# Shared key and value buffers in a sliding-window attention kernel, and output weights split by adding transfers

## The chip, the core and the metric

The kernel runs on one NeuronCore of a Trainium2 chip. The core has a matrix engine (TensorE, PE in the profile, with PEld for its weight loads), a vector engine (VectorE, DVE), a scalar engine (ScalarE, ACT), a general engine (GpSimd, POOL) and a sequencer for transfers (SyncE, SP). Transfers are issued in order from the queues of SP, ACT and POOL and are carried out by 16 DMA engines. The metric is the time of one execution on the device in microseconds (us); lower is better.

## What is computed

The input `x` has 2048 tokens of 512 channels. Two branches are computed from it and mixed by a gate for each token.

```python
q, k, v = split(x @ wqkv)                 # 32 heads of 16 channels
idx = pos[:, None] - off[None, :]         # 8 keys per token, 2 apart, back in time
logits = einsum("bhsd,bhswd->bhsw", q, k[idx]) * scale   # masked where idx < 0
a = einsum("bhsw,bhswd->bhsd", softmax(logits), v[idx]) @ wo
b = (gelu(x @ w_gate) * (x @ w_up)) @ w_down             # hidden width 1792
g = sigmoid((x * gate_w).sum(-1))
out = g * a + (1 - g) * b
```

All numbers are 32 bit floats.

## The kernel before

**Precision.** TensorE multiplies a rounded format, `float32r`. Each operand is split into a high part (the rounded number, a copy on ACT) and a low part (number minus high part), and each product is made of three matmuls: high by high, low by high, high by low. The low part is made in one of two ways. `split` (L83) and `lo` (L787) subtract on DVE. `operands` (L376) and `down_w` (L415) do it with a transfer: ACT writes the negated, rounded number into the place of the low part, and a transfer from POOL's queue adds the full number to it (`accum_op=add`); what is left is the low part.

**Parities.** Since the keys of a token are 2, 4, ... 14 tokens back, even and odd tokens never meet in the attention. The kernel treats them as two parities, 0 and 1, of 1024 tokens each, one behind the other: `start` makes the keys and queries of parity 0, `ffn(0)` runs the hidden layer of parity 0, `kq_second` makes keys and queries of parity 1, and `ffn(1)` runs the hidden layer of parity 1, `out_first` the output product of parity 0, and `finish` that of parity 1. The matmuls of keys and queries and of the hidden layer are arranged as 2 by 2 blocks with seven products in place of eight (names `t1` to `t4`, `s1` to `s4`).

**The hidden layer.** `ffn(par)` goes over 14 blocks `f` of weights. For each, the weights are fetched by SP (`fetch`, L356; in parity 1 the sums made before come back by `fetch_sums`, L409), combined on DVE (`combine`, L367), and split (`operands`). `gate_up` (L494) makes the products of the block; `copy`, `add` and `hidden` (L435 to L450) take them from the PSUM banks. `down` (L464) multiplies pairs of finished blocks by the down weights. In the first two blocks of each parity the values of the attention are made as well (`values`, L174, stored by `take`, L158, through staging tiles `hh`, `hl` and `c`).

**The attention.** It runs on DVE, with its exponential on ACT, beside the matmuls. Each parity has four units `u` of 8 heads (128 channels). A partition holds 8 tokens of a parity in a row and the 7 before them, so keys and values of a unit have 15 slots of 128 channels and queries have 8. For each unit:

- `load_kq` (L185) loads keys (two transfers, `load_slots`, L195) and queries (one) from DRAM into a tile `kq` of 23 slots. For unit 0 they are there already: `take_first` (L137) copies them from PSUM straight into the tile, and `shift` (L148) fetches the 7 earlier slots from the neighbouring partition, after a memset of the first partition's on POOL.
- `scores` (L207) makes four products of 2048 columns (L212) and sums (L215) into `lg`, of which there are two buffers.
- `softmax` (L223), `gated` (L239), and `mix` (L249), which loads the values into a tile `v` of 15 slots, makes four products (L260) with their sums (L264 to L268) into `o`, transposes on DVE into `tb` (L273) and stores to DRAM (L275).

Tiles come from a pool. `kq`, `v`, `tb` and `prod` have one buffer each, so each new tile of such a name waits until all readers of the last one are done. In `start` the buffers of `v`, `tb` and `prod` hold raw weights.

**What sets the order.** `attention` (L296) is a generator that lists the units' steps, each with a price in us; `pull` (L338) is called between the matmuls and takes as many steps as its budget pays for. The steps get a lower priority than the matmuls' own work (`BEHIND`, 150 places), and the products L212 and L260 are tied to the matmul last issued (`paced`). From priorities, dependencies and a simulated timeline a scheduler then sets the order on each engine and each queue; there is no order written out by hand for the attention.

The attention's list begins with `load_kq(0, 0)`, `scores(0, 0)`, `load_kq(0, 1)`, `scores(0, 1)`. After that the next unit's loads come ahead of a unit's `mix` and its scores behind it. At the parity's border the list is: `load_kq(1, 0)`, `scores(1, 0)`, `load_kq(1, 1)`, `softmax(1, 0)`, `scores(1, 1)`.

**The output weights.** `fetch_o` (L649) loads `wo` from POOL's queue during the last block but one of parity 1. `load_o` (L655) splits its four chunks (`WO[u]`) in the last block, with `split` on DVE, into a buffer `g1` (chunks 0 and 1) and two pairs of `S`. `channels_of` and `channels` (L666, L680) then load and split the attention's result, also with `split`; `by_unit` (L689) makes the output's matmuls at L693.

Of the kernel before, what the change touches and what calls it, by code (L numbers as in the profile page):

```python
# [10 lines left out]
F32 = mybir.dt.float32  # L11
F32R = mybir.dt.float32r
AF = mybir.ActivationFunctionType
OP = mybir.AluOpType
AX = mybir.AxisListType

P = 128
# [31 lines left out]
def tile_gated_mix(ctx: ExitStack, tc: tile.TileContext, xt, wqkv, wff, wo, out):  # L49
# [33 lines left out]
    def split(eng, hi, lo, raw, copy=None):  # L83
        if copy:
            copy(hi, raw)
        else:
            nc.scalar.activation(hi, raw, AF.Copy)
        eng.tensor_tensor(lo, raw, hi.bitcast(F32), op=OP.subtract)
# [47 lines left out]

    def take_first(par, ps, jj, copy):  # L137

        if par not in KQ:
            KQ[par] = pool.tile([P, 3 * NP - 1, UC], F32, name="kq")  # L140
        st = tl(next(stages))[:, :CU].rearrange("p (a d) -> p a d", a=2)
        two = ps.rearrange("p (a c d) -> p c a d", a=2, c=2)
        copy(KQ[par][:, NP - 1 + jj::NP], two[:, 0])
        copy(st, two[:, 1])
        for a, t in enumerate((KS[par, 0][1, W:], QS[par, 0][1])):
            nc.sync.dma_start(t.rearrange("(p j) d -> j p d", j=NP)[jj], st[:, a])

    def shift(par, queue, i, j):  # L148
        k = KQ[par][:, :2 * NP - 1]
        if not i:  # L150
            nc.gpsimd.memset(k[:1, :NP - 1], 0.0)
        for a, b in (1, P - 15), (P - 15, P):
            queue.dma_start(k[a:b, i:j], k[a - 1:b - 1, NP + i:NP + j])
# [28 lines left out]

    LG = {}

    def load_kq(par, u):  # L185
        hh, c = divmod(u, 2)
        kq = KQ[par] if not u else pool.tile([P, 3 * NP - 1, UC], F32, name="kq")
        k, q = kq[:, :2 * NP - 1], kq[:, 2 * NP - 1:]
        LG[par, u] = k, q
        if not u:  # L190
            return
        load_slots(k, KS[par, hh][c])
        nc.sync.dma_start(q, QS[par, hh][c].rearrange("(p j) d -> p j d", j=NP))
# [13 lines left out]
    def scores(par, u):  # L207
        k, q = LG[par, u]
        lg = pool.tile([P, UH, NP, W], F32, name="lg", bufs=2)
        for jj in range(0, NP, 2):  # L210
            prod = pool.tile([P, 2, W, UC], F32, name="prod")
            paced(nc.vector.tensor_tensor(prod, spans(k, jj), q[:, jj:jj + 2, None, :].to_broadcast([P, 2, W, UC]),  # L212
                                          op=OP.mult))
            yield 2.3
            nc.vector.tensor_reduce(two_of(lg, jj), prod.rearrange("p j w (h d) -> p (j w) h d", d=DH), axis=AX.X,  # L215
                                    op=OP.add)
            yield 2.3
        first = lg[:1, :, :NP - 1, :W - 1]
        nc.vector.tensor_tensor(first, first, mask[:1, None, :NP - 1, :W - 1].to_broadcast([1, UH, NP - 1, W - 1]),
                                op=OP.min)  # L220
        LG[par, u] = lg
# [27 lines left out]
    def mix(par, u, pause):  # L249
        lg = LG.pop((par, u))  # L250
        hh, c = divmod(u, 2)
        v = pool.tile([P, 2 * NP - 1, UC], F32, name="v")
        load_slots(v, VS[par, hh][c])
        yield pause
        tb = pool.tile([P, 2, BT * UC], F32, name="tb")
        for jj in range(0, NP, 2):
            if jj % BT == 0:
                o = pool.tile([P, 4, BT, 32], F32, name="o")
            prod = pool.tile([P, 2, W, UC], F32, name="prod")
            paced(nc.vector.tensor_tensor(prod.rearrange("p j w (h d) -> p (j w) h d", d=DH),  # L260
                                          spans(v, jj).rearrange("p j w (h d) -> p j w h d", d=DH),
                                          two_of(lg, jj)[:, :, :, None].to_broadcast([P, 2 * W, UH, DH]), op=OP.mult))
            yield 2.3
            nc.vector.tensor_tensor(prod[:, :, :4], prod[:, :, :4], prod[:, :, 4:], op=OP.add)  # L264
            yield 1.2
            nc.vector.tensor_tensor(prod[:, :, :2], prod[:, :, :2], prod[:, :, 2:4], op=OP.add)
            two = [prod[:, :, i].rearrange("p j (b c) -> p b j c", b=4) for i in range(2)]
            nc.vector.tensor_tensor(o[:, :, jj % BT:jj % BT + 2], *two, op=OP.add)  # L268
            yield 1.1

            if jj % BT == BT - 2:
                t = tb[:, jj // BT]
                nc.vector.transpose(t, o.rearrange("p b t c -> p (b t c)"))  # L273
                for a in range(4):
                    nc.sync.dma_start(OS[par, u, jj // BT][:, :, a].rearrange("b i c -> i b c"),  # L275
                                      t[32 * a:32 * a + 32].rearrange("p (b c) -> p b c", b=4))
                yield 0.7
# [18 lines left out]
    def attention():  # L296
        units = [(0, u) for u in range(NU)] + [(1, u) for u in range(NU)]
        yield from need(0, 0)
        load_kq(0, 0)
        yield from scores(0, 0)  # L300
        load_kq(0, 1)
        yield from scores(0, 1)
        yield from need(0, 1)
        scored, mixed = 2, False
        for i, un in enumerate(units):
            if scored == i:
                yield from need(un[0], un[1] // 2 * 2)
                load_kq(*un)
                if un[1]:
                    yield LOAD  # L310
                yield from scores(*un)
                scored += 1
                mixed = False
            if un == (1, 0):
                load_kq(*units[scored])
            yield from softmax(*un)
            if un == (1, 0):
                yield from scores(*units[scored])
                scored += 1
                yield from need(un[0], 1)  # L320
            yield from gated(*un)


            to = units[scored] if scored < len(units) else None
            ahead = to and (to[0], to[1] // 2 * 2) in done
            if ahead:
                load_kq(*to)
            yield from mix(*un, LOAD if mixed else 0.0)
            done.add((*un, "o"))
            mixed = not ahead  # L330
            if ahead:
                yield from scores(*to)
                scored += 1
# [101 lines left out]
    def copy(ps):  # L435
        s = tl("s")
        COPIED[:] = [nc.scalar.activation(s, ps, AF.Copy)]  # L437
        return s
# [216 lines left out]
    def load_o():  # L655
        t = tl("g1", F32R)
        cols = [t[:, i * 512:(i + 1) * 512] for i in range(4)]
        for u in range(NU):
            raw = WO[u]
            WO[u] = hi, lo = pair("S") if u > 1 else cols[2 * u:2 * u + 2]  # L660
            split(nc.vector, hi, lo, raw)
            yield

    OR = []
# [580 lines left out]
```

## Time and profile before

| | |
|---|---|
| median of 3 runs | 600.98 us (600.16 to 601.4) |
| the profiled execution, its own time | 602.86 us |
| its span, first to last instruction | 601.0 us |
| granted TensorE clock | 1.00 |
| TensorE matmul, weight load | 591.8 us (98%), 493.1 us (82%) |
| VectorE | 531.1 us (88%) |
| ScalarE | 391.9 us (65%) |
| GpSimd | 89.3 us (15%) |
| DMA | 134.18 MB, mean 223 GB/s |

How to read it: busy times are of one profiled execution. The span is shorter than the execution's own time by what lies before the first and behind the last instruction. Most waits of an engine other than TensorE cost nothing as long as TensorE is busy meanwhile. Names on the left of an arrow are the tile written, names on its right the tile read; `kq<-ks` is a key load, `kq<-qs` a query load, `v<-vs` a value load, `os<-tb` a store of the attention's result, `raw<-wff` a fetch of hidden weights, `g<-raw` and `d<-r` the making of their parts. L760 is the line of a helper through which many operations of `start` and `kq_second` go.

### The profile page before, as it was taken

How to read it: one execution, taken by the hardware profiler on the slowest of the kernel's cores; microseconds unless marked ns; L12 is line 12 of the kernel's file. 1: busy time of each engine (PE TensorE's matmuls, PEld its weight loads, DVE VectorE, ACT ScalarE, POOL GpSimd, SP SyncE). 2: the span in 40 equal slices, each digit the busy share in tenths (PEclk: the TensorE clock that was granted, in tenths of full speed). 3: DMA queues.
4: the chain of work that ended last, by engine and by line, in shares of the span. 5: the costliest groups of instructions: out<-in, count | busy, mean ns of one | idle time of the engine just before them, and what ended most of it. 6: DMA issues, size and time to landing. Idle time of an engine off the chain costs nothing.

```text
span 601.0 us, 8207 instructions
## 1 busy us (share of the span) xinstructions
PE 591.8 (98%) x2778; PEld 493.1 (82%) x2778; DVE 531.1 (88%) x618; ACT 391.9 (65%) x670; POOL 89.3 (15%) x121
## 2 busy tenths in 40 slices
PE   8999999999999999999999999999999999999997
PEld 6889987788888787888889988788888888888886
DVE  5997969999898897899989887999999988799862
ACT  6845657787678766787772375667667656885532
POOL 0501001111111111202026001111111111101300
PEclk9999999999999999999999999999999999999999
DMA  8789896999889989887879858597867877648924
GB/s 318 259 250 248 242 266 187 265 256 249 241 241 258 232 236 253 223 262 279 282 221 302 219 155 282 144 245 195 238 172 216 214 226 171 168 106 227 159 68 155
DMA packets 80449, 134.18 MB, mean 223 GB/s; under 512 B 8092, under 2 KB 46362, under 8 KB 80152
## 3 DMA queue, kind: packets, MB, share of 16 engines
q1 hardware_dynamic: 62890, 97.67, 50.3%
q0 software_dynamic: 12576, 32.97, 27.5%
q10 hardware_dynamic: 4942, 3.01, 1.6%
q8 instruction: 22, 0.36, 0.3%
q14 instruction: 19, 0.16, 0.1%
HBM read 68.30 MB, written 38.86 MB: 178 GB/s over the span
## 4 chain that ended last, share of the span: by engine, by line
PE 65%; DMA 12%; issue 11%; DVE 7%; ACT 2%; SPq 1%; POOL 1%; ACTq 0%; POOLq 0%; DVEq 0%
PE p L432 26%; PE p L475 9%; PE acc L475 8%; PE acc L760 6%; PE p L693 5%; PE p L760 5%; PE acc L130 4%; DMA d<-r 3%; DMA kq<-qs 3%; DMA ws<-g 3%; DVE prod L212 3%; PE acc L693 2%; DVE lg L215 1%; DMA g<-raw 1%; DMA vs<-hl 1%
## 5 line engine op out<-in xcount | busy, mean ns | idle before, releaser
L432 PE MATMUL p<-S,g 128*128 128x512 f32 x672 | 166.8, 390 | 0.5 <-ACT s L437 0.4
L432 PEld LDWEIGHTS p<-S,g 128*128 128x128 f32 x672 | 125.4, 188 | 27.2 <-ACT s L437 0.8
L432 PE MATMUL p<-A,g 128*128 128x512 f32 x504 | 127.2, 390 | 0.1
L432 PEld LDWEIGHTS p<-A,g 128*128 128x128 f32 x504 | 94.1, 188 | 20.6 <-DVE c L442 1.1
L212 DVE TENSOR_TENSOR prod<-kq 128x2048 f32<-128x2048 f32 x32 | 73.1, 2284 | 16.6 <-DMA kq<-qs 7.7
L390 POOL DMA_DIRECT2D g<-raw x40 | 34.6, 865 | 300.5 <-ACT g L389 230.1
L260 DVE TENSOR_TENSOR prod<-v,lg 128x2048 f32<-128x2048 f32 x32 | 72.9, 2277 | 2.3 <-DMA v<-vs 1.4
L215 DVE TENSOR_REDUCE lg<-prod 128x128 f32<-128x2048 f32 x32 | 73.0, 2281 | 0.2
L475 PE MATMUL p<-d,hh 128*128 128x512 f32 x224 | 68.1, 390 | 0.3 <-ACT hh L448 0.3
L475 PE MATMUL acc<-d,hh 128*128 128x512 f32 x224 | 60.7, 391 | 1.8 <-DMA d<-r 1.8
L475 PEld LDWEIGHTS acc<-d,hh 128*128 128x128 f32 x224 | 41.8, 188 | 11.6 <-DMA d<-r 2.6
L475 PEld LDWEIGHTS p<-d,hh 128*128 128x128 f32 x224 | 42.0, 188 | 9.5 <-ACT hh L448 0.8
L394 ACT ACTIVATE g<-raw 128x1024 fp32r<-128x1024 f32 (+1 forms) x40 | 39.5, 989 | 13.4 <-PE p L432 13.4
L389 ACT ACTIVATE g<-raw 128x1024 fp32r<-128x1024 f32 (+1 forms) x40 | 39.4, 985 | 10.9 <-PE p L760 4.6
L442 DVE TENSOR_TENSOR c<-p,s 128x512 f32<-128x512 f32 x56 | 38.0, 681 | 9.2 <-PE p L432 8.4
L448 ACT ACTIVATE hh<-c 128x512 fp32r<-128x512 f32 x56 | 35.0, 625 | 15.5 <-DVE c L446 15.0
L437 ACT ACTIVATE s<-p 128x512 f32<-128x512 f32 x56 | 33.1, 593 | 18.0 <-PE p L432 16.5
L475 PE MATMUL p<-d,hl 128*128 128x512 f32 x112 | 42.7, 390 | 1.0 <-DVE hl L449 1.0
L449 DVE TENSOR_TENSOR hl<-c,hh 128x512 fp32r<-128x512 f32 x56 | 38.3, 683 | 3.1 <-ACT hh L448 3.0
L446 DVE TENSOR_TENSOR c<-c 128x512 f32<-128x512 f32 x56 | 38.2, 682 | 2.1 <-ACT c L543 1.8
L264 DVE TENSOR_TENSOR prod<-prod 128x1024 f32<-128x1024 f32 x32 | 39.0, 1218 | 0.3
L491 ACT ACTIVATE rt<-p 128x512 f32<-128x512 f32 x48 | 28.2, 593 | 15.3 <-PE p L475 15.2
(180 smaller groups left out, 929.5 us busy)
## 6 DMA issues: line engine op xcount, KB each, us to landing
g<-raw POOLq DMA_DIRECT2D x27, 512.0 KB, 6.8
raw<-wff SPq DMA_DIRECT2D x42, 256.0 KB, 3.4
ws<-g SPq DMA_DIRECT2D x14, 768.0 KB, 6.1
g<-ws SPq DMA_DIRECT2D x14, 768.0 KB, 5.5
r<-wff SPq DMA_DIRECT2D x28, 256.0 KB, 4.3
d<-r POOLq DMA_DIRECT2D x24, 256.0 KB, 6.9
g<-raw POOLq DMA_DIRECT2D x13, 384.0 KB, 6.0
v<-vs SPq DMA_DIRECT2D x8, 512.0 KB, 5.7
```

The source lines that it names most:

```text
L212: paced(nc.vector.tensor_tensor(prod, spans(k, jj), q[:, jj:jj + 2, None, :].to_broadcast([P, 2, W, UC]), op=OP.mult))
L215: nc.vector.tensor_reduce(two_of(lg, jj), prod.rearrange("p j w (h d) -> p (j w) h d", d=DH), axis=AX.X, op=OP.add)
L260: paced(nc.vector.tensor_tensor(prod.rearrange("p j w (h d) -> p (j w) h d", d=DH), spans(v, jj).rearrange("p j w (h d) -> p j w h d", d=D ...
L264: nc.vector.tensor_tensor(prod[:, :, :4], prod[:, :, :4], prod[:, :, 4:], op=OP.add)
L389: nc.scalar.activation(lo, raw, AF.Copy, scale=-1.0)
L394: ins = nc.scalar.activation(hi, raw, AF.Copy)
L432: LAST[:] = [nc.tensor.matmul(ps, w_, a_, start=(start and kc == 0 and n == 0), stop=(kc == 1 and n == 2), skip_group_check=True)]
L446: nc.vector.tensor_tensor(ge, ge, up, op=OP.mult)
L449: nc.vector.tensor_tensor(hl_, ge, hh_.bitcast(F32), op=OP.subtract)
L475: ins = nc.tensor.matmul(pp, a[:, ts], w, start=(i == 0 and n == 0 and gr == 0), stop=(i == 1 and n == 2), skip_group_check=True)
L693: ins = nc.tensor.matmul(pa, a, b, start=(first and n == 0), stop=(last and n == 2), skip_group_check=True)
L760: return lambda *args, **kw: self.add(getattr(self.eng, name)(*args, **kw))
```

## The change

It has two parts.

**Shared buffers.** There are two lasting tiles in place of one per load: `KQ["a"]` of 23 slots (named `kq`) and `KQ["b"]` of 15 slots (named `v`). Keys of unit 0 are in `a` and those of units 1 to 3 in `b`. Queries are in `a`'s last 8 slots, but those of unit 1 go into a `tb` tile. Values of units 0 to 2 are loaded into `a`'s first 15 slots and those of unit 3 into `b`. With this `load_kq(par, 1)` stands ahead of `scores(par, 0)` in the list, in both parities. Parity 1's first keys and queries are copied into the same tile `a` as parity 0's.

**Output weights.** `load_o` makes the low part of each chunk as `operands` does: a negating copy on ACT, an adding transfer from POOL, then the high copy on ACT; the subtraction on DVE goes.

```diff
     def take_first(par, ps, jj, copy):
 
-        if par not in KQ:
-            KQ[par] = pool.tile([P, 3 * NP - 1, UC], F32, name="kq")
+        if "a" not in KQ:
+            KQ["a"] = pool.tile([P, 3 * NP - 1, UC], F32, name="kq")
...
-        copy(KQ[par][:, NP - 1 + jj::NP], two[:, 0])
+        copy(KQ["a"][:, NP - 1 + jj::NP], two[:, 0])
...
     def shift(par, queue, i, j):
-        k = KQ[par][:, :2 * NP - 1]
+        k = KQ["a"][:, :2 * NP - 1]
...
+    def slots_of(other):
+        if not other:
+            return KQ["a"][:, :2 * NP - 1]
+        if "b" not in KQ:
+            KQ["b"] = pool.tile([P, 2 * NP - 1, UC], F32, name="v")
+        return KQ["b"]
+
     def load_kq(par, u):
         hh, c = divmod(u, 2)
-        kq = KQ[par] if not u else pool.tile([P, 3 * NP - 1, UC], F32, name="kq")
-        k, q = kq[:, :2 * NP - 1], kq[:, 2 * NP - 1:]
+        k, q = slots_of(u > 0), KQ["a"][:, 2 * NP - 1:]
+        if u == 1:
+            q = pool.tile([P, 2, BT * UC], F32, name="tb").rearrange("p a (b c) -> p (a b) c", c=UC)
...
     def mix(par, u, pause):
         lg = LG.pop((par, u))
         hh, c = divmod(u, 2)
-        v = pool.tile([P, 2 * NP - 1, UC], F32, name="v")
+        v = slots_of(u == NU - 1)
         load_slots(v, VS[par, hh][c])
...
         yield from need(0, 0)
         load_kq(0, 0)
+        load_kq(0, 1)
         yield from scores(0, 0)
-        load_kq(0, 1)
         yield from scores(0, 1)
...
                 if un[1]:
                     yield LOAD
+                else:
+                    load_kq(un[0], 1)
                 yield from scores(*un)
...
-            if un == (1, 0):
-                load_kq(*units[scored])
             yield from softmax(*un)
...
             WO[u] = hi, lo = pair("S") if u > 1 else cols[2 * u:2 * u + 2]
-            split(nc.vector, hi, lo, raw)
+            nc.scalar.activation(lo, raw, AF.Copy, scale=-1.0)
+            nc.gpsimd.dma_start(lo.bitcast(F32), raw, accum_op=OP.add)
+            nc.scalar.activation(hi, raw, AF.Copy)
             yield
```

## The prediction

> **What bounds the kernel now.** I read the page's totals first, then the 15 us windows, the waits of TensorE, and the timelines of DVE, ACT, POOL and SP around the places that the change touches.
>
> ```profile
> span 601.0 us, 8207 instructions
> PE 591.8 (98%) x2778; PEld 493.1 (82%) x2778; DVE 531.1 (88%) x618; ACT 391.9 (65%) x670; POOL 89.3 (15%) x121
> ...
> 75.00:90.00 15.00, 14.58 (x72) 12.06 (x72) 10.23 (x12) 7.66 (x14) 0.85 (x1) 1.00 0.92 262
> 90.00:105.00 15.00, 14.66 (x65) 11.59 (x64) 14.98 (x20) 10.91 (x16) 2.54 (x3) 1.00 0.67 194
> 195.00:210.00 15.00, 14.38 (x64) 11.59 (x63) 13.23 (x18) 10.73 (x17) 2.57 (x3) 1.00 0.92 234
> 225.00:240.00 15.00, 13.85 (x61) 11.18 (x60) 11.82 (x11) 10.27 (x16) 2.57 (x3) 1.00 1.02 256
> 375.00:390.00 15.00, 13.85 (x59) 10.63 (x58) 15.00 (x14) 9.32 (x15) 1.69 (x2) 1.00 0.60 144
> ```
>
> A window row gives the length, then the busy time (and count) of PE, PEld, DVE, ACT and POOL, the granted clock, the DMA share and GB/s. TensorE is the bound: 601.0 - 591.8 = 9.2 us of it are idle in the whole span, at a granted clock of 1.00. The windows say where: 15 less the first busy time is 0.42 in 75 to 90, 0.34 in 90 to 105, 0.62 in 195 to 210, 1.15 in 225 to 240 and 1.15 in 375 to 390, together 3.7 us; the other 5.5 lie at the two ends (first inputs, last evictions and stores). The change adds and removes no matmul, so idle time is all that it can win, and the middle's 3.7 us is what buffers and loads can reach.
>
> ```profile
> PE acc L475 <- DMA d<-r: 1.8, 2, 1.2
> PE p L475 <- DVE hl L449: 1.0, 1, 1.0
> PE p L432 <- ACT s L437: 0.4, 1, 0.4
> ...
> DVE prod L212 <- DMA kq<-qs: 7.7, 2, 4.6
> ```
>
> The numbers are total, count and longest of each wait. The 1.8 us for `d<-r` are the windows at 195 and 225; `hl` is 375, `s` is 75. The last row is the wait that the change is aimed at: DVE stood 7.7 us for a second unit's keys and queries, once in each parity. It is DVE's wait, not TensorE's.
>
> **The early loads.** Where these stalls are, and what releases them:
>
> ```profile
> 46.65 0.69 DVE L760 TENSOR_TENSOR d<-v,d 128x514 fp32r<-128x514 f32 x1
> 81.80 2.29 DVE L212 TENSOR_TENSOR prod<-kq 128x2048 f32<-128x2048 f32 x1 [4.56 <-DMA kq<-qs]
> 329.50 2.29 DVE L260 TENSOR_TENSOR prod<-v,lg 128x2048 f32<-128x2048 f32 x1
> 369.36 2.29 DVE L212 TENSOR_TENSOR prod<-kq 128x2048 f32<-128x2048 f32 x1 [3.14 <-DMA kq<-qs]
> 377.69 0.69 DVE L449 TENSOR_TENSOR hl<-c,hh 128x512 fp32r<-128x512 f32 x1
> ...
> 52.30 0.43 SPq L146 DMA_DIRECT2D qs<-hl  x1
> 53.25 1.19 SPq L360 DMA_DIRECT2D raw<-wff  x1
> 66.52 0.37 SPq L360 DMA_DIRECT2D raw<-wff  x1
> 71.80 0.32 SPq L196 DMA_DIRECT2D kq<-ks  x1
> ...
> DMA to landing us min/median/max: 1.7/3.6/4.8
> ...
> DMA to landing us min/median/max: 6.5/8.1/8.1
> ```
>
> A row has start, duration and, in brackets, the idle time before it; the two landing rows are L146's stores up to 54 and the key and query loads at 71. In parity 0 the load goes out at 71.80, when the last product of the first scores has read the only key buffer. In the changed kernel its keys go to the value buffer (last read at 46.65 plus 0.69) and its queries to `tb`, free at about that time too. What then ends last is the landing of the stores of L146: 52.30 + 4.8 = 57. With 8.1 us of landing the load is there by 65 to 67, ahead of 77.2 (81.80 - 4.56), where DVE began to wait. The 4.56 us on DVE go. In parity 1 the keys can start when the last mix of parity 0 has read its values, 329.50 + 2.29 = 331.8, and the queries a few us later, when `tb`'s last rows are stored; both are needed at 369.36 - 3.14 = 366.2. The 3.14 us go.
>
> What that is worth on TensorE. At 377.69 DVE is up to 3.14 us early, and PE waited 1.0 us for just that `hl` and 0.15 more in the same window: 1.15 gained (bounds 0, if paced products fill the gap ahead of it, and 1.15). At 83 it is ACT:
>
> ```profile
> 81.89 0.39 ACT L160 ACTIVATE c<-acc 128x256 f32<-128x256 f32 x1 [2.88 <-DMA vs<-c]
> 83.59 0.60 ACT L437 ACTIVATE s<-p 128x512 f32<-128x512 f32 x1
> ```
>
> ACT stood 2.88 us because a stored value tile had not landed, while 1.5 MB of keys and queries were under way from 71.8 to 81.7; the `s` copy queued behind it is what PE waited for. With the keys gone from there the store lands sooner, and 2.88 is well over 0.42: gained 0.42 (bounds 0 and 0.42). The 0.34 behind 90 hang on an ACT queue that holds the first softmax, which moves with the scores: I take 0 (bounds a loss and a gain of 0.34). DVE's freed time itself ends in slack, since its products wait for TensorE's pace. The two `d<-r` waits have neighbours that do not move (weights, and a value load that still waits for the mix before): I take their 1.77 as staying, with bounds of 0 and twice that, since they hang on which transfers meet.
>
> On SP the moved load stands behind the fetch of 53.25, and behind it nothing is issued before 66.52. In parity 1 the query load may hold value stores and weight fetches back on SP until `tb` is stored, a few us; no wait of TensorE stands in any of the windows from 240 to 375, so I take 0 (bounds 0 and 1.0). The bytes are the same, and the last values of each parity find their buffer free earlier as well.
>
> **The shared buffer.** First keys, all queries but one, and the values of units 0 to 2 lie in one tile, so parity 1's first writes must wait for the third mix of parity 0:
>
> ```profile
> 245.27 0.84 POOL L151 MEMSET kq<- 1x896 f32 x1 [10.47 <-DVE prod L212]
> 286.14 2.28 DVE L260 TENSOR_TENSOR prod<-v,lg 128x2048 f32<-128x2048 f32 x1
> 298.31 0.38 ACT L760 ACTIVATE kq<-p 128x256 f32<-128x256 f32 x1
> ```
>
> That mix ends its reading at 288.4. The copy comes at 298.31: 9.9 us of slack, nothing. The memset moves from 245 to 288 or behind; its value is read by the shifts, which follow the copies. Queued behind it on POOL are, at worst, the parity's output stores, for whose tiles nobody waits in this trace: 0 (bounds 0 and 1.0).
>
> **The output weights.** Four subtractions of DVE go; four negating copies on ACT and four POOL transfers come.
>
> ```profile
> 532.96 1.14 ACT L87 ACTIVATE g<-raw 128x512 fp32r<-128x512 f32 x2
> 535.00 0.58 ACT L437 ACTIVATE s<-p 128x512 f32<-128x512 f32 x1
> 540.75 0.60 ACT L491 ACTIVATE rt<-p 128x512 f32<-128x512 f32 x1 [0.97 <-PE p L475]
> ...
> 532.28 0.68 DVE L88 TENSOR_TENSOR A<-raw,A 128x512 fp32r<-128x512 f32 x1
> ...
> 532.31 0.85 POOL L419 DMA_DIRECT2D d<-r  x1 [9.07 <-ACT d L418]
> DMA to landing us min/median/max: 3.9/3.9/3.9
> ...
> 537.83 1.52 PE L432 MATMUL p<-S,g 128*128 128x512 f32 x6
> 544.17 1.52 PE L693 MATMUL p<-g,A 128*128 128x512 f32 x6
> ```
>
> From 532.96 on ACT runs without a gap to 539.8 (540.75 - 0.97). Two copies of this shape take 1.14 us, so the second adds 0.52, and four add 2.1 us there. The tightest taker is the `s` copy of 535.00: it ends at 535.58, and the product that overwrites its bank starts at 537.83, so 2.25 us of slack against 2.1. I cost it at nothing, with 1.0 as the far bound if other copies gather ahead of it too. The low parts: the first negation can stand where the first `g` copy stands, and its transfer (like that of 532.31, 3.9 us from issue to landing) is there by 538; the fourth, some 4 us later, by 542. TensorE wants the first at 544.4 and the fourth, ten matmuls on at 0.23 to 0.25 each (six in 1.52), at 546.4. Cover 4 us; without it the 3.9 of one transfer would show. DVE's four subtractions (0.68 each as in the row of 532.28, so 2.7) lie where PE waits for nothing: worth 0.
>
> The Trainium skill warns of this very move in "SBUF — State Buffer" (SBUF: two separate sides): a transfer issued from GpSimd cannot write its descriptors while VectorE, in an operation of the kind that takes both ports, holds the pair they share. If each were held for one VectorE operation of 2.3 us, the fourth would land 9 us later and TensorE would stand some 5 us. The issue of 532.31 took 0.85 us beside the subtraction of 532.28, so the trace speaks against it and it gets no chance of its own.
>
> **Sum.** The profiled execution took 602.86 us by its own time, 601.0 of span and 1.86 around it; gains 1.15 + 0.42 = 1.6, costs 0, so it would take 601.3. It stands 1.88 over the median of the runs, 600.98; taken from the median the forecast is 599.4.
>
> **Rivals.** *Hidden anyway* (0.20): DVE is early, but its order changes with the loads, so that another late sum takes the place of `hl`, and the short ACT wait only shifts. For it: DVE is full (15.00 of 15) in the very window of 375, so its queue is long whoever is early. Against it: 3.14 us early against 1.0. Time 600.7.
>
> *The early keys crowd the weights* (0.25, slower). Place: 54 to 66, where DMA is nearly full:
>
> ```profile
> 54.00:57.00 3.00, 1.00 1.08 248
> 66.00:69.00 3.00, 1.00 0.32 87
> ...
> 62.58 0.69 DVE L371 TENSOR_TENSOR raw<-raw 128x512 f32<-128x512 f32 x1 [0.28 <-DMA vs<-hl]
> 65.39 0.68 DVE L442 TENSOR_TENSOR c<-p,s 128x512 f32<-128x512 f32 x1
> 68.37 1.55 PE L432 MATMUL p<-S,g 128*128 128x512 f32 x6
> ```
>
> (Length, clock, DMA share, GB/s.) The sum of 62.58 reads the weights fetched from 53.25 on, and DVE already stood 0.28 us before it. If the 1.5 MB (6 us at 250 GB/s) get among them, this sum and all of DVE behind it start up to 6 us late; the sum of 65.39, which frees a bank, ends at 66.1 and has 2.3 us before a product may want that bank at 68.37. It decides from 2.3 us of delay on; at the full 6 PE loses 3.7 and keeps only the 1.15 gained at 375: 600.98 + 3.7 - 1.15 = 603.5. Halfway it is 602. Against it: the load cannot start before about 57, and DMA has room behind (0.32 from 66). The Trainium skill, "DMA: Bandwidth & Descriptors" (Queues, rings and completion order), has each DMA engine take one queue's descriptors in ring order; by that, fetches issued earlier on SP's queue stay ahead and this rival dies.
>
> *More than forecast* (0.15): the `d<-r` waits go as well, as transfers meet otherwise, nearly all of 1.77: 599.4 - 1.5 = 597.9.
>
> **Chances.** The forecast has 0.40. 0.2% (1.2 us) is about what a measurement of this kernel can tell from no change. Faster by more than that: most of the forecast (its own range is 598.9 to 600.2) and all of "more", 0.48 together. Within it: "hidden", the forecast's rest and a little of "crowded", 0.26. Slower: 0.26, the rest of "crowded" and the far bounds of the small costs above. The range 597.8 to 603.0 leaves out the far end of "crowded" and little below.
>
> **What would show it.** Right: the wait of L212 for `kq<-qs` gone, keys issued near 57 and 332, window 375 to 390 with PE at 15.0, no PE wait in 75 to 90, no wait of L693 on a `g` or `S` transfer. Wrong: a DVE idle at L371 near 62, a PE wait in 537 to 547, or POOL standing at the memset with weight transfers behind it.

## The result, and the profile after

| | median of runs | lowest to highest |
|---|---|---|
| before | 601.72 us (21 runs) | 599.24 to 603.37 |
| changed | 603.90 us (21 runs) | 601.11 to 607.18 |

The changed kernel takes 1.0039 times the time before (95% interval 1.0023 to 1.0055): slower by 2.2 us by the medians. Its profiled execution took 606.6 us, with a span of 604.8 and a granted clock of 0.997, so it is one of the longer ones; the reading below says where such an execution loses its time, and the experiments how much of that other executions pay. Single executions that lie far off, one of e9 below at 2122 us and three of the kernel before at 819 to 850, are left out of all ratios.

The totals of the changed kernel, and its windows of 15 us that answer to those before, with two of 3 us (length, busy PE, PEld, DVE, ACT, POOL, clock, DMA share, GB/s):

```profile
PE 593.8 (98%) x2778; PEld 494.0 (82%) x2778; DVE 528.4 (87%) x614; ACT 394.1 (65%) x674; POOL 92.8 (15%) x125
```

```profile
75.00:90.00 15.00, 11.56 (x54) 9.46 (x54) 11.24 (x9) 7.05 (x16) 0.85 (x1) 0.89 0.74 230
84.00:87.00 3.00, 0.62 (x2) 0.52 (x3) 1.06 (x2) 2.11 (x5) 0.00 (x0) 0.93 0.44 131
87.00:90.00 3.00, 3.00 (x8) 2.33 (x8) 2.21 (x2) 3.00 (x7) 0.85 (x1) 0.50 0.85 265
105.00:120.00 15.00, 14.22 (x63) 11.30 (x62) 14.95 (x21) 10.94 (x19) 4.26 (x5) 1.00 0.90 231
120.00:135.00 15.00, 14.53 (x65) 11.71 (x64) 12.19 (x20) 10.48 (x15) 2.02 (x3) 1.00 0.93 251
375.00:390.00 15.00, 15.00 (x68) 12.32 (x67) 12.03 (x15) 12.20 (x18) 2.57 (x3) 1.00 0.62 159
```

The window at 375 is full, as forecast: its 1.15 us are gained in this execution. The window at 75 has lost 3.44 us of TensorE instead of 0.42, and the clock stands at 0.50 behind it. Two small losses are new, 0.78 at 105 and 0.47 at 120. A third, the wait of 0.61 us for `hh` near 553, looks like chance: the window from 540 to 555 is full in the kernel before and in a second profile of the changed kernel (e11).

TensorE's waits of the changed kernel (total, count, longest):

```profile
PE p L440 <- ACT s L445: 3.4, 1, 3.4
PE p L79 <- DVE zero L73: 1.1, 1, 1.1
PE p L440 <- ACT rt L499: 0.8, 1, 0.8
PE acc L483 <- ACT hh L456: 0.6, 1, 0.6
PE acc L770 <- DVE A L770: 0.6, 1, 0.6
PE acc L483 <- DMA d<-r: 0.5, 1, 0.5
PE p L483 <- ACT p L477: 0.3, 1, 0.3
```

The line numbers of the changed kernel are 8 to 10 above those before (L437 is now L445), and those of the experiments' kernels move again by a few. The wait for `hl` is gone and the `d<-r` waits of the windows at 195 and 225 are all but gone; the wait for `s` is eight times as long.

It is also a wait for another copy. A block of weights has two copies into `s` (`p5` and `u2` in `gate_up`). In the kernel before, TensorE stood 0.42 us for the second, at 83.59. The first had run long before, and the product that adds to its bank came 3.3 us after its end:

```profile
78.41 0.60 ACT L437 ACTIVATE s<-p 128x512 f32<-128x512 f32 x1 [2.36 <-PE p L432]
...
82.30 1.52 PE L432 MATMUL p<-S,g 128*128 128x512 f32 x6
```

In the changed kernel this first copy stands behind the last value copies on ACT, and it is the one that TensorE waits for.

Back from that wait, on the timelines of PE, ACT, SP and DVE of the changed kernel, and then one piece of its chain of waits (start and duration):

```profile
86.38 4.62 PE L440 MATMUL p<-S,g 128*128 128x512 f32 x12 [3.44 <-ACT s L445]
...
66.78 0.37 ACTq L162 DMA_DIRECT2D vs<-hl  x1
67.18 1.28 ACT L535 ACT_TABLE_LOAD   x1 [3.54 <-DMA vs<-hh]
81.40 0.39 ACT L160 ACTIVATE c<-acc 128x256 f32<-128x256 f32 x1 [5.02 <-DMA vs<-c]
83.13 0.38 ACT L160 ACTIVATE c<-acc 128x256 f32<-128x256 f32 x1 [1.29 <-DMA vs<-c]
85.72 0.60 ACT L445 ACTIVATE s<-p 128x512 f32<-128x512 f32 x1 [0.44 <-ACT c L160]
...
55.84 1.38 SPq L204 DMA_DIRECT2D v<-ks  x1
57.27 1.37 SPq L205 DMA_DIRECT2D v<-ks  x1
60.46 0.32 SPq L201 DMA_DIRECT2D tb<-qs  x1
...
64.07 0.68 DVE L379 TENSOR_TENSOR raw<-raw 128x512 f32<-128x512 f32 x1
```

```profile
55.73 10.98 DMA vs<-hh
```

The keys go out at 55.84, in the middle of the first pass's value stores, which ACT issues from 54 on. ACT then stands three times for such a store's landing, 3.54 + 5.02 + 1.29 us, and comes to the first copy into `s` at 85.72 instead of 78.41. The bracket of 67.18 is the wait of the store's issue at 66.78. It waits for an earlier store that counts on the same semaphore: that store was on its way from 55.73 for 10.98 us, to 66.71. The waits on `c` are for a staging tile whose store has not landed.

The landings themselves, for the value stores issued between 53 and 68 us, in the kernel before and then in the changed one, and the DMA share there in the changed one:

```profile
DMA to landing us min/median/max: 2.2/3.8/8.0
```

```profile
DMA to landing us min/median/max: 4.6/8.7/12.4
```

```profile
66.00:69.00 3.00, 3.00 (x27) 3.00 (x26) 3.00 (x4) 1.81 (x3) 0.00 (x0) 1.00 1.07 365
```

The median store lands 4.9 us later, and the share at 66 is 1.07 where it was 0.32. The sum of 64.07 on DVE, in contrast, has no wait: the weights fetched ahead of the keys on SP's queue came in time. The Trainium skill, "DMA: Bandwidth & Descriptors" (Queues, rings and completion order), has each DMA engine take the descriptors of one queue in ring order, and says next to it that the engine takes turns between the queues that have work. The trace agrees with both: the fetches ahead on SP's own queue came in time, and the stores of ACT's queue landed later.

The stall is paid twice. The 12 matmuls behind it take 4.62 us; in an execution without the stall (below) the same 12 take 2.88, so the clock of 0.50 costs 1.74 more. The Trainium skill, "TensorE: Matmul & The Clock Gate" (Part 1), has the clock halve after a window of about 3.4 us without work and come back after as long under load. Here 3.44 us of idling did it, and since 12 matmuls at half the rate would take 5.76 us, the rate was back before their end. A stall of 2.56 us at the same place in e2's profile left the clock at 1.00.

### The profile page after: what moved, and what is told of

Same layout as the page of the kernel before. It is cut to its first block, busy times and chain, and to the rows that moved or that the text cites. A ratio compares the mean times of both kernels' runs of the same rounds, so it can differ in the third digit from the quotient of the medians.

```text
span 604.8 us, 8209 instructions
## 1 busy us (share of the span) xinstructions
PE 593.8 (98%) x2778; PEld 494.0 (82%) x2778; DVE 528.4 (87%) x614; ACT 394.1 (65%) x674; POOL 92.8 (15%) x125
## 4 chain that ended last, share of the span: by engine, by line
PE 68%; DMA 14%; ACT 3%; issue 3%; DVE 2%; ACTq 0%; SPq 0%; POOL 0%; POOLq 0%; DVEq 0%
PE p L440 32%; PE acc L483 10%; PE p L483 10%; PE p L703 4%; PE acc L130 4%; PE acc L770 4%; DMA d<-r 3%; PE p L770 3%; DMA ws<-raw 2%; DMA vs<-hh 2%; PE acc L703 2%; DMA g<-raw 2%; DMA vs<-c 1%; DMA raw<-os 1%; DMA raw<-xt 1%
## 5 line engine op out<-in xcount | busy, mean ns | idle before, releaser
L483 PE MATMUL acc<-d,hh 128*128 128x512 f32 x224 | 59.3, 391 | 1.2 <-ACT hh L456 0.6
L268 DVE TENSOR_TENSOR prod<-kq,lg 128x2048 f32<-128x2048 f32 x24 | 54.7, 2278 | 0.3
L445 ACT ACTIVATE s<-p 128x512 f32<-128x512 f32 x56 | 33.1, 593 | 18.8 <-PE p L440 15.1
L220 DVE TENSOR_TENSOR prod<-v,kq 128x2048 f32<-128x2048 f32 x16 | 36.5, 2281 | 3.2 <-PE p L440 1.7
L130 PE MATMUL acc<-d,A 128*128 128x256 f32 (+1 forms) x288 | 37.9, 281 | 0.0
```

What stands on the lines that cost most here:

```text
L130: LAST[:] = [nc.tensor.matmul(ps[:, :cn], a[:, t], w[:, c0:c0 + cn], start=(kc == 0 and n == 0), stop=(kc == KC - 1 and n == 2))]
L483: ins = nc.tensor.matmul(pp, a[:, ts], w, start=(i == 0 and n == 0 and gr == 0), stop=(i == 1 and n == 2), skip_group_check=True)
```

## The experiments

Theory A: the first pass's early keys and queries crowd the value stores, ACT comes late, and TensorE pays. Theory B: the output weights' low parts are the loss. Theory C: the sharing of the buffers as such. Theory D, formed later: the order of the instructions, which the scheduler drew up anew, and not the bytes. The runs of the table were made on different chips, so a small difference of two medians is to be read with the ratios beside it. All ratios are to the kernel before, run on the same chip beside each.

| run | what it is | median us | ratio, 95% interval |
|---|---|---|---|
| e1_lowparts | before, with the new low parts | 601.68 | 1.0013 (0.9998 to 1.0028) |
| e2_buffers | changed, with the old low parts | 603.46 | 1.0046 (1.0028 to 1.0064) |
| e3_hold0 | changed, first pass's loads late | 600.42 | 0.9985 (0.9972 to 0.9998) |
| e4_sp_stores | changed, first value stores from SP | 602.44 | 1.0018 (1.0004 to 1.0031) |
| e5_hold01 | changed, both passes' loads late | 602.06 | 1.0011 (0.9996 to 1.0025) |
| e6_thin | changed, an eighth of the early bytes | 601.67 | 1.0004 (0.9986 to 1.0023) |
| e7_mid | changed, early loads 6 us later | 601.30 | 1.0003 (0.9986 to 1.0020) |
| e8_hold0_split | e3 with the old low parts | 600.26 | 0.9982 (0.9966 to 0.9997) |
| e9_s_first | changed, `s` ahead of the last `c` | 603.0 to 604.9, five runs | 1.0049 (1.0029 to 1.0068) |
| e10_s_last | e3, `s` behind the last `c` | 600.46 | 0.9985 (0.9973 to 0.9997) |
| e11_change | the changed kernel again | 604.83 | 1.0055 (1.0034 to 1.0075) |
| e12_twice | e3 with the early bytes added | 606.26 | 1.0079 (1.0054 to 1.0104) |

The kernel before had medians of 601.1 to 601.5 in these.

**The two parts of the change apart.** e1 puts the diff's `load_o` into the kernel before; e2 takes it out of the changed kernel:

```diff
-            nc.scalar.activation(lo, raw, AF.Copy, scale=-1.0)
-            nc.gpsimd.dma_start(lo.bitcast(F32), raw, accum_op=OP.add)
-            nc.scalar.activation(hi, raw, AF.Copy)
+            split(nc.vector, hi, lo, raw)
```

> The kernel before, with only the output weights' low parts made by negation on ACT, an adding transfer on POOL's queue and a rounding copy on ACT. Theory A (the first pass's early keys and queries crowd the value stores that ACT issues, ACT comes late to the copy into s at 83 us, the TensorE idles 3.4 us there and its clock drops): this kernel lacks that load, so it is level with the kernel before, within 0.6 us (the 0.61 us wait for hh near 553 us that the changed kernel's trace has may appear), and its trace has no wait above 1 us near 83 us. Theory B (the ACT copies and transfers at the end are the loss): slower than before by about the whole 2.2 us. Theory C (the shared buffers as such, by new waits for a buffer): level.

> The changed kernel with the output weights split as before (copy and subtraction on VectorE); the buffers and loads are those of the change. Theory A: the stall at 83 to 86 us and the drop of the granted clock after it stay, time 603.3 to 604 us where the kernel before has 601.7, so slower by 1.6 to 2.3 us. Theory B: the loss is gone and the 1.15 us gained near 380 us show, about 600.6 us. Theory C: as A in time, but the stall at 83 us isn't what carries it.

e1 is level with before, e2 slower by 2.3 us. The low parts are not the loss, and theory B falls. They are no gain either: e1's interval allows from 0.1 us less to 1.7 more, and e8 against e3 shows 0.16 us.

**The first pass's early loads taken back.** e3 puts `load_kq(0, 1)` behind the first scores in the list again. With the shared buffers that alone need not hold the loads back, so they are also made to wait, as the single buffer made them:

```diff
...
+        if u == 1 and par in (0,):
+            for x in loads:
+                after(x, MUL[par, 0])
...
```

`MUL[par, 0]` is the last multiply of the first unit's scores.

> The changed kernel, except that in the first pass the second unit's key and query transfers wait for the last multiply of the first unit's scores, where the kernel before had them; the second pass and the shared buffers are as in the change. Theory A: the wait of TensorE near 83 us falls from 3.44 us to 0.5 us or less, the granted clock of the span is 0.999 or above in every run, and with the gain near 380 us (1.15 us) left the kernel is faster than before by about 1 us: 600.7 us where before has 601.7 (range 600.0 to 601.5). Theory B: stays at about 603.5 us. Theory C (sharing as such, or the third unit's queries, which still go early): stays slower than before, 602.5 us or more, with the clock at 0.997 in part of the runs.

The time came as theory A had it, 600.42, and faster than before by 0.9 us. All 12 runs have a clock of 0.999 or 1.0. On PE and DVE of this kernel:

```profile
82.59 2.88 PE L444 MATMUL p<-S,g 128*128 128x512 f32 x12
...
82.00 2.29 DVE L223 TENSOR_TENSOR prod<-v,tb 128x2048 f32<-128x2048 f32 x1 [4.70 <-DMA tb<-qs]
```

The 12 matmuls have no wait ahead of them. DVE stands its 4.70 us for the second unit's queries again, as it did before the change (4.56), and the kernel is the faster one: in the first pass that wait cost TensorE nothing that shows. It also speaks against theory C, since the sharing and the third unit's early queries are in this kernel too.

**The second pass.** e5 holds the loads in both passes, `par in (0, 1)`, and has the list's old order in both.

> The changed kernel with the second unit's key and query transfers held behind the last multiply of the first unit's scores in both passes: of the change only the shared buffers and the low parts are left. Theory A (the loss is the first pass's early transfers, the gain is the second pass's): VectorE's hl wait of about 1 us between 375 and 390 us is back, so 0.6 to 1.2 us slower than the kernel that holds them in the first pass alone (600.42 us): 601.0 to 601.8 us, level with before. Rival: the gain of that kernel comes from the sharing itself, not from the second pass's early load: then 600.4 us again.

The time is 1.64 us above e3's, somewhat more than expected. DVE's waits of the two kernels, e3 and then e5 (total, count, longest):

```profile
DVE prod L223 <- DMA tb<-qs: 4.7, 1, 4.7
```

```profile
DVE prod L223 <- DMA tb<-qs: 6.4, 2, 4.6
```

The second pass's wait of DVE is back, with 1.8 us. The `hl` wait of TensorE is not in the one profile of e5, and the window where it would stand is fuller there than in e3. First e5, then e3:

```profile
375.00:390.00 15.00, 14.85 (x65) 11.70 (x64) 15.00 (x16) 8.74 (x15) 1.69 (x2) 1.00 0.81 181
```

```profile
375.00:390.00 15.00, 14.35 (x64) 11.57 (x63) 14.89 (x13) 9.14 (x15) 2.54 (x3) 1.00 0.67 148
```

That execution of e5, 600.69 us, is nearly the shortest of its 12. So the times show that the second pass's early load, with the order that came with it, is worth something (1.6 us, 0.8 to 2.3 by the spread of the two sets of runs). Where an ordinary execution of e5 pays isn't shown, and bytes and order were not told apart in this pass.

**Bytes or order.** With the early loads come other orders on PE, DVE, ACT and SP. e6 keeps every order of the changed kernel and cuts the bytes: the early transfers carry 16 of 128 partitions, two memsets on POOL fill the tiles, and the second unit's scores are of other data.

```diff
-        load_slots(k, KS[par, hh][c])
...
+        n = 16 if (par, u) == (0, 1) else P
+        if n < P:
+            nc.gpsimd.memset(k, 0.0)
+            nc.gpsimd.memset(q, 0.0)
+        load_slots(k, KS[par, hh][c], n)
...
```

> The changed kernel, except that the first pass's early key and query transfers (second unit) carry 16 of the 128 partitions; the rest of the two tiles is filled by two memsets on POOL, so the second unit's scores are of other data. Each queue and engine has its instructions in the order of the changed kernel. Theory A (the bytes of 1.5 MB crowd the value stores): the wait for s near 83 us is below 0.6 us and the clock of every run at 0.999 or above; the two small waits that every kernel with this load has shown (0.8 us for rt near 112 us, 0.4 us for d near 127 us) stay, since they'd come of the order: 600.5 to 601.5 us. Rival D (it is the order of the queues and the semaphores that the transfers share, not the bytes): the wait near 83 us stays at 2 us or more, and the time at 603 us or above.

e12 does the reverse. It keeps every order of e3 and adds the three transfers where the change has them; the second unit reads the later load.

```diff
...
+        load_slots(k, KS[0, 0][1])
+        nc.sync.dma_start(t, QS[0, 0][1].rearrange("(p j) d -> p j d", j=NP))
...
+        yield from scores(0, 0)
         load_kq(0, 1)
...
```

> The kernel that holds the early transfers in the first pass (600.42 us), with the same three transfers (second unit's keys and queries of the first pass, 1.5 MB) issued twice: once early, where the change has them, and once more where that kernel holds them; the second unit's scores read the second load. The rest of every engine's and queue's order is that kernel's. Theory A (early bytes crowd the value stores): the loss of the bytes comes back without the change's order: ACT waits for the value stores' landings, the TensorE waits for s near 83 us in part of the runs, time 602.5 to 604 us, some runs at a clock of 0.997 or below. Theory D (the changed order alone): 600.4 to 600.9 us, clock at 0.999 or above.

Without seven eighths of the bytes the time is 601.67, every clock is 0.999 or 1.0, and the median is 2.2 us below the changed kernel's first 21 runs (603.90) and 3.2 below its 12 runs of e11 (604.83). With the bytes in the good order it is 606.26, above what theory A had given, with five clocks of six at 0.997 or below. The stall of e12, on PE and ACT:

```profile
87.44 4.62 PE L450 MATMUL p<-S,g 128*128 128x512 f32 x12 [3.41 <-ACT s L455]
...
66.08 0.37 ACTq L162 DMA_DIRECT2D vs<-hl  x1
85.09 0.38 ACT L160 ACTIVATE c<-acc 128x256 f32<-128x256 f32 x1 [5.17 <-DMA vs<-c]
86.80 0.60 ACT L455 ACTIVATE s<-p 128x512 f32<-128x512 f32 x1 [0.38 <-ACT z L164]
```

It is the changed kernel's stall to 0.03 us, for the same first copy into `s`, with the same 4.62 us of slow matmuls. Here that copy has e3's place, ahead of the last value copy. The bytes make the long stall. The transfers of e12 cross twice, so its 5.8 us over e3 is not the size of the change's loss. And theory A missed in one point: e6's profile, one of its longer executions (603.07 us), still has 1.5 us of waiting for `s`. The second profile of the changed kernel, of an execution of 603.96 us in e11, has less. First e6, then e11:

```profile
PE p L444 <- ACT s L449: 1.5, 2, 1.2
```

```profile
PE p L440 <- ACT s L445: 1.1, 2, 0.8
```

So it is not single profiles but the times and clocks of 12 runs each that tell e6 from the changed kernel. The landings are no better: the median in e6's profile is 5.5 us, between the 3.8 before and the 8.7 of the changed kernel, but e10 below, without early transfers and without a stall, has 5.8, and e13, with only a short one, 8.0.

Between e6 and e3 lie another 1.25 us, which the two intervals of the ratios hardly tell from nothing. The windows of 105 and 120 tell them, in e6 first and then in e3:

```profile
105.00:120.00 15.00, 14.22 (x63) 11.40 (x62) 14.97 (x18) 10.28 (x16) 3.42 (x4) 1.00 1.03 268
120.00:135.00 15.00, 14.73 (x66) 11.86 (x65) 11.67 (x20) 11.47 (x19) 2.57 (x3) 1.00 0.90 230
```

```profile
105.00:120.00 15.00, 14.96 (x65) 11.71 (x64) 15.00 (x20) 10.57 (x17) 2.57 (x3) 1.00 1.00 267
120.00:135.00 15.00, 15.00 (x68) 12.31 (x67) 14.47 (x23) 12.91 (x20) 2.60 (x3) 1.00 0.85 218
```

TensorE idles 0.78 + 0.27 us in e6 and 0.04 in e3. The 0.78 is in every profile with the changed order (the changed kernel twice, e2, e4, e6, e7, and the second look at e9) and in none with another; e12, with the bytes in e3's order, has 0.15 there. So this part goes with the order; which of its many exchanges does it was not taken apart.

**The place of one copy.** In the changed order the first copy into `s` stands behind the last value copy instead of ahead of it. e9 moves it ahead in the changed kernel, by emitting the last value copy after it; e10 moves it behind in e3.

```diff
...
+            ordered(take(LASTC.pop(), 0, NP - 1, 1, tag="c"), COPIED[-1])
...
         p5 = copy(Z_)
+        last_take()
...
```

```diff
...
         p5 = copy(Z_)
+        if not par and f == 1:
+            ordered(COPIED[-1], LASTC[-1])
...
```

> The changed kernel with one instruction moved: on ACT the first copy into s stands ahead of the first pass's last value copy, as in the kernel before, instead of behind it. Early transfers and stores are those of the change. Theory D (that the planner put s behind a copy that waits for a staging tile is the loss): the wait near 83 us falls below 1 us, the clock stays at 0.999 or above, 601 to 602 us. Theory A (ACT is late as a whole, by the landings of several stores: its copies of 81.40 and 83.13 us in the changed kernel's trace each ended a wait): s moves by one copy and one store issue, 0.9 us, so the wait stays near 2.5 us, and only the clock may be spared: 602.5 to 603.5 us.

> The kernel that holds the early transfers in the first pass (600.42 us), with the first copy into s put behind the first pass's last value copy, as in the changed kernel; everything else in the same order. Theory A: the staging tile of that copy came free at 80.08 us there, so s comes about 1.8 us later than 78.70 us; the TensorE waits 0.3 to 1.5 us, the time is 600.5 to 601.8 us. Theory D: the wait is as in the changed kernel, 2.5 us or more, and the time 602.5 us or above.

> The changed kernel itself again, on the same chip and beside the same runs of the kernel before as the two others. All theories: 602.9 to 604 us. If the stall at 83 us sets the clock back only when it lasts longer than about 3 us, the runs fall in two groups, those at a clock of 0.997 or below some 1.7 us slower on average than those at 0.999 or above.

e9 kept the loss and e10 did not get it, so this place, the first candidate of theory D, does not make the loss. e11 came in above its 602.9 to 604, and its two groups lie 2.8 us apart and not 1.7 (below). e9 was run once more for its profile.

> The changed kernel with the first copy into s ahead of the last value copy, once more for its profile. Theory A: ACT's copies into c between 73 and 84 us wait several us in sum for the landing of the value stores, and the wait for s near 83 us is at most 0.9 us shorter than it would be behind the last copy; like the changed kernel's, it varies from run to run (3.4 us in one profile, 1.1 us in the other). Theory D: no wait for s above 0.5 us.

That execution was a short one, 600.79 us. ACT of it:

```profile
64.09 1.28 ACT L547 ACT_TABLE_LOAD   x1 [0.43 <-ACT hl L160]
73.68 0.39 ACT L160 ACTIVATE c<-acc 128x256 f32<-128x256 f32 x1 [0.51 <-DMA vs<-c]
79.72 0.39 ACT L160 ACTIVATE c<-acc 128x256 f32<-128x256 f32 x1 [5.59 <-DMA vs<-c]
81.43 0.60 ACT L456 ACTIVATE s<-p 128x512 f32<-128x512 f32 x1 [0.38 <-ACT z L164]
```

The wait of 5.59 us for a staging tile is as long as in the changed kernel, yet the first `s` comes at 81.43, in time, and TensorE waits only 0.67 us, for the second. What is missing is the wait at 64 to 67: the store ahead of the table load went out without one here, where ACT stood 3.54 us in the changed kernel and 5.52 at a store of 66.08 in e12. The six profiles that have the changed order, and ACT as the issuer of the stores, go together in this (us; the waits at staging tiles are added up from 73 us to the first `s`):

| profile | ACT's wait at the store | at staging tiles | first `s` starts | TensorE's wait for it |
|---|---|---|---|---|
| changed | 3.54 | 6.31 | 85.72 | 3.44 |
| e2 | 3.55 | 6.14 | 84.98 | 2.56 |
| e6 | 2.20 | 5.72 | 83.20 | 1.20 |
| e11 | 1.69 | 5.98 | 82.90 | 0.84 |
| e7 | 0.84 | 5.90 | 82.63 | none |
| e13 | none | 6.10 | 81.43 | none |

The waits at the staging tiles are much the same in all six, with an eighth of the bytes too, so the early bytes hardly make these; what does was not taken apart. A late store at 61 to 67 shifts all of ACT behind it, and together with the later 6 us TensorE feels it. That is the likeliest reason why the executions differ; it was read in these profiles and not tested by itself. In the 21 runs of the changed kernel the ten with a clock of 0.997 or below have a mean of 605.4 us and the other eleven 602.8; in e11 six and six, 605.7 and 602.9. The groups overlap: a run of 603.3 us is among the ten and one of 605.8 among the eleven.

**Two ways round it.** e4 issues the first pass's value stores from SP, so that ACT does not stand at a store:

```diff
-        (nc.sync if par else nc.scalar).dma_start(rows(VS[par, hh][:, W:], jj), two)
+        nc.sync.dma_start(rows(VS[par, hh][:, W:], jj), two)
```

> The changed kernel, except that the first pass's value stores are issued by SP's queue instead of ACT's. Theory A as the trace was first read (ACT is held at the store instruction itself, since each transfer of the hardware queues waits for an earlier one that counts on the same semaphore): ACT no longer waits there, the wait near 83 us falls below 1 us, the clock stays at 0.999 or above, time 600.5 to 601.5 us against 601.7. Theory A2 (ACT is held because the four small staging tiles aren't free until their stores have landed, whoever issues them): the wait near 83 us stays at 2 us or more and the time stays at 603 us or above. A new loss is possible too: SP issues in order, and the raw weight fetches then stand behind the stores; VectorE's subtractions near 64 us would show waits for raw.

e7 lets the early loads wait for the second of the four multiplies.

> The changed kernel, except that the first pass's early transfers wait for the second of the first unit's four multiplies, which ended at 61.8 us in the changed kernel's trace, so they start some 6 us later than there and 10 us earlier than in the kernel before; the order on SP is that of the changed kernel. Theory A, if only the stores of 55 to 61 us are the victims: the wait for s near 83 us falls below 1 us, the time to 600.5 to 601.5 us. If every store up to 76 us suffers, as the wait of 5.02 us for the store of 74 us in the changed kernel's trace suggests: the wait stays at 2 us or more, 602.5 us or above.

ACT of e4, and then of e7:

```profile
75.15 0.39 ACT L160 ACTIVATE c<-acc 128x256 f32<-128x256 f32 x1 [1.69 <-DMA vs<-c]
79.20 0.39 ACT L160 ACTIVATE c<-acc 128x256 f32<-128x256 f32 x1 [2.91 <-DMA vs<-c]
79.48 0.59 ACT L445 ACTIVATE s<-p 128x512 f32<-128x512 f32 x1
```

```profile
63.70 0.37 ACTq L162 DMA_DIRECT2D vs<-hl  x1
64.09 1.28 ACT L539 ACT_TABLE_LOAD   x1 [0.84 <-DMA vs<-hh]
80.04 0.38 ACT L160 ACTIVATE c<-acc 128x256 f32<-128x256 f32 x1 [5.90 <-DMA vs<-c]
82.63 0.60 ACT L449 ACTIVATE s<-p 128x512 f32<-128x512 f32 x1 [0.44 <-ACT c L160]
```

In both the wait for `s` is at most 0.3 us in the profile and every clock is 0.999 or above. In e7 the 5.90 us wait is there in full, but the one at 64 has shrunk from 3.54 to 0.84: it is the stores of 55 to 61 us that count, as the first half of its expectation had it. e4's 602.44 is above what theory A gave, and still 2 us above e3. Of these 1.2 are the waits of the order (0.78 + 0.45 in its profile, a short execution of 599.8 us); what makes the rest isn't shown.

**The better kernel.** e8 is e3 with the old low parts.

> The kernel that holds the early transfers in the first pass (600.42 us), with the output weights split as before on VectorE instead of by adding transfers. If the low parts cost what the kernel with them alone showed (0.47 us over before, interval from -0.1 to 1.7): 600.0 us (599.4 to 600.5), faster than before by 1.3 us. If their cost there was chance: 600.4 us again.

At 600.26 us it is faster than before by 1.1 us by its ratio, and within 0.2 us of e3. It keeps of the change only the shared buffers and the second pass's early loads.

## Why the prediction was wrong

The forecast was 599.4 us in a range of 597.8 to 603.0; the change takes 603.9 and is slower.

- *The window of 375, 1.15 gained.* The size is borne out roughly, the place is not. DVE's two waits for the second unit's loads are gone, as forecast, and in the changed profile the window is full; e5 against e3 puts the second pass's early load at 1.6 us. But the window has 0.56 us of idling in the changed kernel of e11 and 0.65 in e3, both with the early load, and 0.15 in e5 without it. That the `hl` wait carries the gain is not shown.
- *The copy into `s` at 83, 0.42 gained.* This is the step that failed: "With the keys gone from there the store lands sooner, and 2.88 is well over 0.42: gained 0.42 (bounds 0 and 0.42)". The keys were gone from 72 to 82 us, and were now among the stores of 55 to 68. I followed the load to its new place for the weights only, and not for the stores that ACT issues there and then waits for. The later store did not land sooner either: ACT stood 5.02 and 1.29 us for staging tiles where it had stood 2.88. And I priced only the second copy into `s`, where the first, with 3.3 us of room, came 7.3 us later. The window lost 3.44 us instead of winning 0.42, and the clock 1.74 more; against e6 most of the bytes cost 2.2 to 3.2 us in the middle run. The bounds shut a loss out, which no row of the trace allowed.
- *The rival of the early keys that crowd the weights (0.25, 602 to 603.5).* Right place, right cause and about the right price, with the wrong victim. DVE and its weights were safe; the value stores were not. The ring order that I let speak against the whole rival bears on SP's own queue and says nothing of ACT's. That its times come so near to the 603.9 is partly luck, since they were worked out for a delay of DVE that did not happen.
- *What lies outside the sum.* I took the order of the engines as staying but for what moves. The new loads led to a new order, and some 0.8 to 1.8 us of idling near 112 and 127 go with it in the profiles.
- *The two `d<-r` waits, 1.77, staying.* They shrank to 0.15 in the changed profile, as the rival "more than forecast" had it, but the same rows move from run to run: e3 has 0.72 in the window at 225 and 0.65 in the one at 375, the changed kernel of e11 0.58 and 0.56, and e1, with the old loads, 0.15 at 225. So nothing here ties them to the change. The 0.34 behind 90, taken as 0, is gone in the changed profile and 0.58 in e11.
- *The costs at nothing.* The memset, and SP's queue in the second pass: right, no wait of TensorE appears there (the changed profile has 0.27 us of idling at 270, ahead of both). ACT's copies for the low parts: right within what e1 and e8 can tell (0 to 0.8 us). No matmul of the changed profile waits on a transfer of them. One sum there is slightly off: ten matmuls of 0.23 to 0.25 us after 544.4 end at 546.7 to 546.9, not at 546.4, which leaves a little more cover.

## What to carry over

A transfer that is moved earlier is to be costed at its new place against everything that is in flight there, other queues' stores above all, and from each of these to the engine that stands for its landing: here 1.5 MB beside small stores made ACT late, not their own reader. A long wait of an engine off the bound is no gain in itself: DVE's 4.7 us in the first pass were free, and the load that ended its 3.1 us in the second was worth about 1.6. A load can be made early where the DMA engines have room by tying it to an instruction that runs then; with the wait of 6 us in e7 two thirds to three quarters of the loss against e3 went, by the ratios.

## What was not expected of the hardware

A stall of TensorE of 3.44 us cost half as much again in clock: 12 matmuls took 4.62 instead of 2.88 us, in the changed kernel and, after 3.41 us, in e12. The stalls of 2.56 us in the profile of e2 and of 0.84 in that of e11 left the clock at 1.00. That may be why the run times of the changed kernel spread over 6 us, and those of the kernels without such a stall over some 3 to 4.5: a stall that is sometimes 3.4 us long and sometimes shorter pays the clock in part of the runs only.
